# Issuing each product over a whole PSUM bank of 512 columns as two halves of 256 columns

## The chip, the cores and the metric

The kernel runs on one core of a Trainium2 chip. The metric is the device time of one execution in microseconds (us). The time before is the median of three runs: 1025.2 us (1024.93 to 1025.28).

## The reference

A gated scan over 6080 tokens of 256 features is followed by two feed-forward layers of 2048 hidden features, one with a leaky ReLU, one with an ELU. Everything is float32.

```python
sig = 1.0 / (1.0 + np.exp(-f_logit))
f = lower_bound + (1.0 - lower_bound) * sig
h = f[:, t] * h + (1.0 - f[:, t]) * x[:, t]     # for every t; y[:, t] = h
...
h = y @ w_in1;  g = np.maximum(0.01 * h, h);                                y = g @ w_out1
h = y @ w_in2;  g = np.where(h > 0.0, h, np.exp(np.minimum(h, 0.0)) - 1.0); out = g @ w_out2
```

## The kernel before

The tokens are worked in 12 chunks (`sizes`): eleven of 512 and, as the fifth, one of 448. Features lie on the partitions, tokens along the columns. A float32 operand is held as two parts in the type float32r, a high part (a rounded copy, made on ScalarE) and a low part (what the copy lost, made on VectorE). A product of two such operands takes three matmuls into the same place in PSUM: high by high, high by low, low by high. `mm3` (lines 572 to 577) issues these three; lines 575, 576 and 577 of the profile are they, for nearly every product of the kernel. The stationary operand of each matmul is a piece of 128 columns of a `w` tile, and each matmul loads it anew (PEld in the profile, LDWEIGHTS). The moving operand is an `act` tile (the input of a layer) or a `gate` tile (the activation's output).

`group(i)` (line 586) handles one entry of `stream`: a layer, a chunk and a quarter of the hidden features, that is two pairs of blocks of hidden features. It has two kinds of products.

- Products inward (`act` tiles). For most chunks `product` forms them by Strassen's scheme with seven products of half the size: the chunk's tokens are split in two halves, so that each matmul has 256 columns (224 in the chunk of 448). Each product is two calls of `mm3`, six matmuls, in one PSUM bank. The first two chunks of layer 1 are computed without the scheme (`plain`), with matmuls over 512 columns, because the combinations of the weights are not there yet.
- Products outward (`gate` tiles). `run` calls `mm3` for the two output blocks (`k`), each over the whole chunk: six matmuls of 512 columns (448 in the one chunk), into two banks. In the last chunk of layer 2 (`swapped`) the output is formed with the roles changed, the gate tile stationary and the weights moving, by lines 734 to 736, 256 columns each.

PSUM has eight banks, six `bank` tiles and two `seed` tiles; each holds 512 float32 columns. ScalarE and VectorE take the products out, apply the activation, and split the result into the high and low part of a gate tile (lines 704 and 707). At the start, VectorE, ScalarE and GpSimd also prepare the weights: they decode them from the words as loaded (lines 346 to 359) and split them (lines 371 and 373); line 463 and line 465 split the input of a plain chunk. While the first chunks run, the weights of layer 1 and the combinations of them are made in this way.

The order of the work on every engine is set by `Plan.emit`, a list scheduler that runs while the kernel is built. Each operation has a cost in microseconds, a due time and the operations that it waits for; the scheduler simulates the engines and issues, for each, the operation that can start and is due first. The costs of matmuls come from one function, which `cost_in` and `cost_out` use for the due times too:

```python
def mm(n):
    return n * 0.000451 + 0.0025
```

With it 256 columns cost 0.1180 us and 512 columns 0.2334 us.

Of the kernel before, what the change touches and what calls it, by code (L numbers as in the profile page):

```python
# [106 lines left out]
def kernel(  # L107
# [21 lines left out]
    nc = tc.nc  # L129
# [10 lines left out]
    CH = 512  # L140
# [29 lines left out]
    HC = CH // 2  # L170
# [24 lines left out]
        return 0.09 + n / 1200.0  # L195

    def mm(n):
        return n * 0.000451 + 0.0025

    DMA, LATE, FAR, SGN = 0.475, 2.3, 4.5, 0.8  # L200

# [25 lines left out]
    def cost_in(n):  # L227
        return 42 * mm(n // 2)

    def cost_out(n):  # L230
        return 24 * mm(n)
# [340 lines left out]
    def mm3(ps, wop, a, start, stop):  # L572


        nc.tensor.matmul(ps, wop[0], a[0], start=start, stop=False, skip_group_check=True)  # L575
        nc.tensor.matmul(ps, wop[0], a[1], start=False, stop=False, skip_group_check=True)  # L576
        nc.tensor.matmul(ps, wop[1], a[0], start=False, stop=stop, skip_group_check=True)  # L577

    y_in = {}
    prods = []  # L580
# [3 lines left out]
    def group(i):  # L584
# [24 lines left out]
        def product(bank, s, t, start, stop, after, **k):  # L609
            def run():  # L610
                for j, p in enumerate(pairs):
                    mm3(ps(bank)[:, j * h : (j + 1) * h], wop(p, s), src["op"](t), start and j == 0, stop)

            o = pe(6 * mm(h), due_in[i] + count[0] * step, run, after + src["done"][t] + wi + prods[-1:], **k)
            count[0] += 1
            prods.append(o)
            return o
# [8 lines left out]
        def plain():  # L626

            blocks = [(r, j) for r in (1, 0) for j in (0, 1)]
            todo = [(r, j, k) for r, j in blocks for k in range(KD)]
            if i < 2:  # L630
                todo.sort(key=lambda t: (t[2], t[1]) if i == 0 else t[2])
            for z, (r, j, k) in enumerate(todo):
                name = f"{r}{j}"

                def run(r=r, j=j, k=k, name=name):
                    s = {(1, 0): A11, (1, 1): A12, (0, 0): A21, (0, 1): A22}[r, k]
                    mm3(b[name][2][:, :n], wop(pairs[j], s), src["row"](k), k == 0, k == KD - 1)

                prods.append(pe(3 * mm(n), due_in[i] + z * step * 7 / 8, run,
                                wplain[pairs[j]] + src["rows"][k] + prods[-1:],  # L640
                                take=[(b, name, "seed" if j else "bank")] if k == 0 else [],
                                give=[(src, "p", "act")] if q == NQ - 1 and z == len(todo) - 1 else []))
                if k == KD - 1:
                    g = "hO" if r else "hE"
                    made.setdefault(r, []).append(act(s1(n), None, lambda j=j, name=name, g=g: nc.scalar.activation(
                        out=b[g][2][:, j * n : (j + 1) * n], in_=b[name][2][:, :n], func=AF.Prelu, alpha=0.01),
                        [prods[-1]], take=[(b, g, "h")] if j == 0 else [], give=[(b, name, "seed" if j else "bank")]))
# [69 lines left out]
        for z, (name, r, j) in enumerate(order):  # L717
            due = due_in[i] + 7 * step * (1.75 + z / 4)
            begin, end = q == 0 and z == 0, q == NQ - 1 and z == 3
            give = [(b, name, "gate")] if j == 1 else []  # L720

            def run(name=name, r=r, j=j, begin=begin, end=end):
                hi, lo = (gate(name, s)[:, j * n : (j + 1) * n] for s in (0, 1))
                wh, wl = wout(pairs[j], r)
                if not swapped:
                    for k in range(KD):
                        cols = slice(k * P, (k + 1) * P)
                        mm3(yb[k][2][:, :n], (wh[:, cols], wl[:, cols]), (hi, lo), begin, end)
                    return

                for t in range(n // P):
                    dst = yb[t // 2][2][:, t % 2 * D : (t % 2 + 1) * D]
                    ah, al = (s[:, t * P : (t + 1) * P] for s in (hi, lo))
                    nc.tensor.matmul(dst, ah, wh, start=begin and t % 2 == 0, stop=False, skip_group_check=True)  # L734
                    nc.tensor.matmul(dst, ah, wl, start=False, stop=False, skip_group_check=True)  # L735
                    nc.tensor.matmul(dst, al, wh, start=False, stop=end, skip_group_check=True)  # L736

            prev = pe(6 * mm(n), due, run, [gates[name], prev] + wo + outs[-1:],
                      take=[(yb, k, "bank") for k in range(KD)] if begin else [], give=give)
            outs.append(prev)  # L740
# [55 lines left out]
    for sd in seeds:  # L796
        for z in range(CH // P):
            nc.tensor.matmul(sd[:, z * P : (z + 1) * P], ident, ident, start=z == 0, stop=z == CH // P - 1,
                             skip_group_check=True)
# [67 lines left out]
```

## Time and profile before

| | |
|---|---|
| median of three runs | 1025.2 us |
| the profiled execution | 1024.31 us |
| its span, first to last instruction | 1022.5 us |
| mean granted TensorE clock | 0.996 |
| matmuls, and as many weight loads | 6336 |
| memory traffic | 47 MB read, 24 MB written, 69 GB/s over the span |

The profiled execution is 0.9 us shorter than the median; 1.8 us of it lie outside the span. PE is the matmul side of TensorE, PEld its weight loads, DVE is VectorE, ACT ScalarE, POOL GpSimd. A matmul's duration in the trace runs from its first read to a modelled end and overlaps the next matmuls, so the busy share of PE only tells that it had something in flight.

### The profile page before, as it was taken

Reading aid. Unit: us, or ns where it says so; the run is one execution under the profiler, and the core shown is the slowest. Engines: PE = TensorE matmul, PEld = TensorE weight load, DVE = VectorE, ACT = ScalarE, POOL = GpSimd, SP = SyncE. Lnnn points to the kernel's source line nnn. Section 1 sums busy time; section 2 is a strip of 40 time slices with the busy share of each in tenths; the row PEclk is TensorE's granted clock in tenths of the full one; section 3 lists DMA queues with packets and bytes.
Section 4 is the critical chain, followed back from the end, with each engine's and each line's share of the span. In section 5 each row is a group of like instructions: output and inputs, shape, how many; then the busy total and the mean of one; then the engine's idle time right before and its main releaser. Section 6 shows DMA issues by size and latency. Waiting matters only on the chain.

```text
span 1022.5 us, 15868 instructions
## 1 busy us (share of the span) xinstructions
PE 1009.5 (99%) x6336; PEld 901.7 (88%) x6336; DVE 758.5 (74%) x1061; ACT 714.9 (70%) x1038; POOL 36.6 (4%) x38
## 2 busy tenths in 40 slices
PE   7999999999999999999999999999999999999998
PEld 5777889999888888888898888889989888888997
DVE  7899867768779688474377776877777768787765
ACT  6776767777778677666577676766776767676664
POOL 2132000000000000000000000000000000000000
PEclk8999999999999999999999999999999999999999
DMA  6532333445264443211760201102102021021010
GB/s 185 134 104 62 76 90 93 129 98 140 59 150 104 124 93 103 40 50 40 281 214 2 42 1 39 42 1 43 27 14 42 1 42 42 2 42 16 7 21 21
DMA packets 155290, 71.99 MB, mean 70 GB/s; under 512 B 132176, under 2 KB 145488, under 8 KB 155216
## 3 DMA queue, kind: packets, MB, share of 16 engines
q1 hardware_dynamic: 155216, 70.98, 26.7%
q8 instruction: 49, 0.80, 0.3%
q14 instruction: 25, 0.20, 0.1%
HBM read 46.97 MB, written 23.99 MB: 69 GB/s over the span
## 4 chain that ended last, share of the span: by engine, by line
PE 89%; DVE 5%; ACT 2%; issue 2%; DMA 1%; SPq 1%; POOL 1%; DVEq 0%; ACTq 0%
PE bank L575 27%; PE bank L576 27%; PE bank L577 27%; PE seed L577 2%; PE seed L576 2%; PE seed L575 2%; DVE ws L359 1%; DVE ws L355 1%; ACT gate L704 1%; POOL ws L349 1%; DVE gate L707 1%; PE bank L736 1%; PE bank L734 0%; PE bank L735 0%; DVE w L373 0%
## 5 line engine op out<-in xcount | busy, mean ns | idle before, releaser
L575 PE MATMUL bank<-act,w 128*128 128x256 f32 (+2 forms) x1088 | 306.6, 282 | 0.4 <-ACT act L463 0.2
L576 PE MATMUL bank<-act,w 128*128 128x256 f32 (+2 forms) x1088 | 304.6, 280 | 1.3 <-DVE act L465 1.3
L577 PE MATMUL bank<-act,w 128*128 128x256 f32 (+2 forms) x1088 | 304.4, 280 | 0.0
L576 PE MATMUL bank<-gate,w 128*128 128x512 f32 (+1 forms) x736 | 289.1, 393 | 0.0
L577 PE MATMUL bank<-gate,w 128*128 128x512 f32 (+1 forms) x736 | 288.9, 393 | 0.0
L575 PE MATMUL bank<-gate,w 128*128 128x512 f32 (+1 forms) x736 | 287.9, 391 | 0.0
L623 DVE TENSOR_TENSOR h<-bank,sn 128x512 f32<-128x512 f32 (+1 forms) x176 | 120.3, 684 | 186.5 <-ACT sn L620 101.1
L576 PEld LDWEIGHTS bank<-act,w 128*128 128x128 f32 x1088 | 204.8, 188 | 18.5 <-DVE act L465 2.3
L575 PEld LDWEIGHTS bank<-act,w 128*128 128x128 f32 x1088 | 204.9, 188 | 17.6 <-ACT sn L620 1.1
L577 PEld LDWEIGHTS bank<-act,w 128*128 128x128 f32 x1088 | 204.7, 188 | 1.8 <-DVE w L373 0.5
L620 ACT COPY sn<-bank 128x512 f32<-128x512 f32 (+1 forms) x176 | 102.4, 582 | 105.0 <-PE bank L577 104.3
L577 PEld LDWEIGHTS bank<-gate,w 128*128 128x128 f32 x736 | 138.3, 188 | 29.7
L575 PEld LDWEIGHTS bank<-gate,w 128*128 128x128 f32 x736 | 138.4, 188 | 17.7
L576 PEld LDWEIGHTS bank<-gate,w 128*128 128x128 f32 x736 | 138.4, 188 | 16.0
L707 DVE TENSOR_TENSOR gate<-h,gate 128x1024 fp32r<-128x1024 f32 (+1 forms) x96 | 117.3, 1222 | 33.6 <-ACT gate L704 33.2
L707 DVE TENSOR_TENSOR gate<-ws,gate 128x1024 fp32r<-128x1024 f32 (+1 forms) x96 | 113.2, 1210 | 10.2 <-ACT gate L704 10.2
L704 ACT CAST gate<-h 128x1024 fp32r<-128x1024 f32 (+1 forms) x96 | 99.9, 1040 | 3.7 <-PE bank L577 1.9
L704 ACT CAST gate<-ws 128x1024 fp32r<-128x1024 f32 (+1 forms) x96 | 96.2, 1038 | 4.1 <-DVE ws L685 2.8
L679 ACT ACTIVATE ws<-bank 128x512 f32<-128x512 f32 (+1 forms) x48 | 28.5, 594 | 70.9 <-PE bank L577 70.9
L575 PE MATMUL seed<-act,w 128*128 128x256 f32 (+2 forms) x208 | 61.5, 296 | 0.8 <-ACT w L371 0.5
L577 PE MATMUL seed<-act,w 128*128 128x256 f32 (+2 forms) x208 | 61.4, 295 | 0.6 <-DVE w L373 0.4
L692 ACT ACTIVATE ws<-ws 128x1024 f32<-128x1024 f32 (+1 forms) x48 | 50.5, 1052 | 15.9 <-DVE ws L689 15.8
(72 smaller groups left out, 1159.9 us busy)
## 6 DMA issues: line engine op xcount, KB each, us to landing
ws<-in_moe_w_in_dram SPq DMA_DIRECT2D x32, 255.6 KB, 3.7
ws<-in_moe_w_out_dram SPq DMA_DIRECT2D x32, 255.6 KB, 3.5
w2d<-gate SPq DMA_DIRECT2D x8, 896.0 KB, 4.3
w<-w2d SPq DMA_DIRECT2D x8, 896.0 KB, 6.0
y1d<-t SPq DMA_DIRECT2D x22, 256.0 KB, 2.2
bt<-y1d SPq DMA_DIRECT2D x22, 256.0 KB, 2.9
out_dram<-t SPq DMA_DIRECT2D x80, 64.0 KB, 2.0
raw<-in_f_logit_dram SPq DMA_DIRECT2D x72, 64.0 KB, 3.1
```

Source lines behind the costliest of these rows:

```text
L349: sg = pool(SGN, None, lambda: nc.gpsimd.tensor_scalar(out=fr(), in0=top().bitcast(I8), scalar1=2.0, scalar2=-2.0, op0=ALU.min, op1=ALU.ma ...
L355: fm = dve(v1(n), None, lambda: nc.vector.scalar_tensor_tensor(out=fr().bitcast(I32), in0=mant(), scalar=5, in1=fr().bitcast(I32), op0=ALU ...
L359: mu = dve(v1(n), None, lambda: nc.vector.tensor_tensor(out=val()[:, :n], in0=fr(), in1=sc(), op=ALU.mult,), [fm, ex])
L575: nc.tensor.matmul(ps, wop[0], a[0], start=start, stop=False, skip_group_check=True)
L576: nc.tensor.matmul(ps, wop[0], a[1], start=False, stop=False, skip_group_check=True)
L577: nc.tensor.matmul(ps, wop[1], a[0], start=False, stop=stop, skip_group_check=True)
L620: return act(s1(2 * h), None, lambda: nc.scalar.copy(out=ps(name), in_=ps("X")), after, take=[(b, name, "sn")])
L623: return dve(v1(2 * h), None, lambda: nc.vector.tensor_tensor(out=half(name, s), in0=two(ps(bank)), in1=two(ps(sn)), op=ALU.add), after, **k)
L679: a, o = (act(s1(2 * h), None, lambda s=s, name=name: nc.scalar.activation(out=half("eO", s), in_=two(ps(name)), func=AF.Relu, scale=-1.0) ...
L692: e = act(s1(2 * n), None, lambda: nc.scalar.activation(out=whole("eE"), in_=whole("eE"), func=AF.Exp, scale=-1.0), [e])
L704: hi = act(s1(2 * n), None, lambda name=name, g=g: nc.scalar.copy(out=gate(name, 0), in_=whole(g)), done + highs[-1:], take=[(b, name, "ga ...
L707: gates[name] = dve(v1(2 * n), None, lambda name=name, g=g: nc.vector.tensor_tensor(out=gate(name, 1), in0=whole(g), in1=gate(name, 0).bit ...
```

## The change

`mm3` looks at the number of columns. Below 512 it issues its three matmuls as before. At 512 it issues the three for the columns 0 to 255 and then the three for the columns 256 to 511, into the same bank. Only the very first matmul of a bank carries the start mark. Each matmul loads its stationary operand itself, so the weight loads double with the matmuls. The cost function gets two new values, 0.1136 us for 256 columns and 0.2272 us for 512; other sizes keep theirs (448 columns 0.2045 us, 224 columns 0.1035 us).

```diff
--- before.py
+++ after.py
@@ -195,7 +195,7 @@
         return 0.09 + n / 1200.0
 
     def mm(n):
-        return n * 0.000451 + 0.0025
+        return (n * 0.000451 + 0.0025 if n < CH else 0.2272) if n != HC else 0.1136
 
     DMA, LATE, FAR, SGN = 0.475, 2.3, 4.5, 0.8
 
@@ -572,9 +572,12 @@
     def mm3(ps, wop, a, start, stop):
 
 
-        nc.tensor.matmul(ps, wop[0], a[0], start=start, stop=False, skip_group_check=True)
-        nc.tensor.matmul(ps, wop[0], a[1], start=False, stop=False, skip_group_check=True)
-        nc.tensor.matmul(ps, wop[1], a[0], start=False, stop=stop, skip_group_check=True)
+        n = ps.shape[-1]
+        parts = [slice(0, n)] if n < CH else [slice(0, HC), slice(HC, CH)]
+        for z, s in enumerate(parts):
+            nc.tensor.matmul(ps[:, s], wop[0], a[0][:, s], start=start and z == 0, stop=False, skip_group_check=True)
+            nc.tensor.matmul(ps[:, s], wop[0], a[1][:, s], start=False, stop=False, skip_group_check=True)
+            nc.tensor.matmul(ps[:, s], wop[1], a[0][:, s], start=False, stop=stop, skip_group_check=True)
 
     y_in = {}
     prods = []
```

The lines behind `mm3` move by three: 575 to 577 become 578 to 580, 704 and 707 become 707 and 710, 734 to 736 become 737 to 739. The program issues 8508 rows of work on TensorE instead of 6300. Since the scheduler works with other costs, the orders of the engines change too.

TensorE in layer 2, an output product of one quarter, before (`bank` tiles are PSUM banks, `gate` the moving operand, `w` the stationary one):

```order
L575 MATMUL bank_103<-gate_111,w_69 128x512
L576 MATMUL bank_103<-gate_111,w_69 128x512
L577 MATMUL bank_103<-gate_111,w_69 128x512
L575 MATMUL bank_104<-gate_111,w_69 128x512
L576 MATMUL bank_104<-gate_111,w_69 128x512
L577 MATMUL bank_104<-gate_111,w_69 128x512
```

and an output product of the same weights now, up to the first matmul of its second bank:

```order
L578 MATMUL bank_100<-gate_111,w_69 128x256
L579 MATMUL bank_100<-gate_111,w_69 128x256
L580 MATMUL bank_100<-gate_111,w_69 128x256
L578 MATMUL bank_100<-gate_111,w_69 128x256
L579 MATMUL bank_100<-gate_111,w_69 128x256
L580 MATMUL bank_100<-gate_111,w_69 128x256
L578 MATMUL bank_101<-gate_111,w_69 128x256
```

What were three matmuls into one bank are six of half the length, three for each half of the bank.

TensorE at the start of layer 1, in the second chunk (`act_107` is its input, `gate_109` the first gate tile of the first chunk), before:

```order
L575 MATMUL seed_99<-act_107,w_64 128x512
L576 MATMUL seed_99<-act_107,w_64 128x512
L577 MATMUL seed_99<-act_107,w_64 128x512
L575 MATMUL bank_105<-gate_109,w_63 128x512
L576 MATMUL bank_105<-gate_109,w_63 128x512
```

These three are the last plain matmuls of the second chunk's first quarter, and the first output product stood behind them. Now:

```order
L578 MATMUL bank_101<-gate_109,w_63 128x256
L579 MATMUL bank_101<-gate_109,w_63 128x256
L580 MATMUL bank_101<-gate_109,w_63 128x256
L578 MATMUL bank_104<-act_107,w_63 128x256
L579 MATMUL bank_104<-act_107,w_63 128x256
L580 MATMUL bank_104<-act_107,w_63 128x256
```

The first output product (its last rows are shown) stands ahead of the plain products that use the second half of the chunk's features.

VectorE at the same place (`act1` is the second chunk's input, `gate0` the first gate tile, `w1` a weight tile, `ws` scratch of the weights' preparation, `bt` and `t` tiles of the scan), before:

```order
L546 SCALAR_TENSOR_TENSOR bt0_108<-t2_129,last_h_94,t0_127 128x512
L359 TENSOR_TENSOR ws0_117<-ws0_117 128x512
L346 TENSOR_SCALAR up0_130<-ws1_118 128x512
L465 TENSOR_TENSOR act1_107<-bt0_108,act1_107 128x512
L355 SCALAR_TENSOR_TENSOR ws2_119<-ws1_118,ws2_119 128x512
L373 TENSOR_TENSOR w1_64<-ws0_117,w1_64 128x512
L707 TENSOR_TENSOR gate0_109<-h0_113,gate0_109 128x1024
```

and now:

```order
L546 SCALAR_TENSOR_TENSOR bt0_108<-t2_129,last_h_94,t0_127 128x512
L346 TENSOR_SCALAR up0_130<-ws1_118 128x512
L373 TENSOR_TENSOR w1_64<-ws0_117,w1_64 128x512
L710 TENSOR_TENSOR gate0_109<-h0_113,gate0_109 128x1024
L355 SCALAR_TENSOR_TENSOR ws0_117<-ws1_118,ws0_117 128x512
L465 TENSOR_TENSOR act1_107<-bt0_108,act1_107 128x512
```

The split of the second chunk's input (line 465) stood ahead of the split of the first gate tile and now stands behind it.

## Rows read from the trace of the kernel before

**Rows 1.** The page's head: span, then busy time of each engine and instructions.
```profile
span 1022.5 us, 15868 instructions
...
PE 1009.5 (99%) x6336; PEld 901.7 (88%) x6336; DVE 758.5 (74%) x1061; ACT 714.9 (70%) x1038; POOL 36.6 (4%) x38
```

**Rows 2.** Table of stretches, the first 100 us; columns as its first line says.
```profile
core 0: us, PE busy (x) PEld busy (x) DVE busy (x) ACT busy (x) POOL busy (x), PEclk, DMA share, GB/s
0.00:25.00 25.00, 19.00 (x81) 14.14 (x81) 17.54 (x28) 15.66 (x28) 5.16 (x11) 0.86 0.64 189
25.00:50.00 25.00, 24.11 (x102) 19.20 (x103) 21.52 (x30) 19.37 (x32) 4.09 (x5) 1.00 0.55 124
50.00:75.00 25.00, 24.85 (x107) 19.70 (x107) 24.44 (x46) 17.64 (x30) 8.42 (x4) 1.00 0.37 107
75.00:100.00 25.00, 24.09 (x103) 18.76 (x102) 24.43 (x50) 17.37 (x31) 6.72 (x3) 1.00 0.34 76
```

**Rows 3.** Table of stretches, TensorE alone: length, busy (count), clock, DMA, GB/s.
```profile
85.30:1011.50 926.20, 926.04 (x5964) 1.00 0.25 64
```

**Rows 4.** The chain that ended last, in order of time: start, length, engine and line.
```profile
84.51 0.61 DVE w L373
85.17 0.50 PE seed L577
```

**Rows 5.** Groups of matmuls by shape, whole span: count | busy us, mean ns | idle before.
```profile
L575 PE MATMUL bank<-act,w 128*128 128x256 f32 x960 | 267.3, 278 | 0.2
...
L575 PE MATMUL bank<-gate,w 128*128 128x512 f32 x672 | 264.4, 393 | 0.0
L575 PE MATMUL seed<-act,w 128*128 128x256 f32 x160 | 44.2, 276 | 0.0
...
L734 PE MATMUL bank<-w,gate 128*128 128x256 f32 x64 | 17.8, 278 | 0.0
...
L575 PE MATMUL bank<-act,w 128*128 128x512 f32 x32 | 13.2, 414 | 0.2 <-ACT act L463 0.2
...
L575 PE MATMUL seed<-act,w 128*128 128x512 f32 x32 | 12.9, 404 | 0.8 <-ACT w L371 0.5 <-ACT h L645 0.3
```

**Rows 6.** The same groups in the first 85.4 us.
```profile
L575 PE MATMUL bank<-gate,w 128*128 128x512 f32 x42 | 16.6, 396 | 0.0
...
L575 PE MATMUL bank<-act,w 128*128 128x512 f32 x26 | 10.9, 418 | 0.2 <-ACT act L463 0.2
...
L575 PE MATMUL seed<-act,w 128*128 128x512 f32 x25 | 10.2, 407 | 0.8 <-ACT w L371 0.5 <-ACT h L645 0.3
```

**Rows 7.** Timeline of TensorE in layer 2: start us, duration us, instruction.
```profile
799.76 0.39 PE L575 MATMUL bank<-gate,w 128*128 128x512 f32 x1
...
801.15 0.28 PE L575 MATMUL bank<-act,w 128*128 128x256 f32 x1
...
802.52 0.39 PE L575 MATMUL bank<-gate,w 128*128 128x512 f32 x1
```

**Rows 8.** The same view, where every matmul has 512 columns, to the first of 256.
```profile
86.21 0.39 PE L575 MATMUL bank<-act,w 128*128 128x512 f32 x1
...
101.61 0.28 PE L575 MATMUL bank<-act,w 128*128 128x256 f32 x1
```

**Rows 9.** The same view, in the chunk of 448 tokens.
```profile
700.30 0.27 PE L575 MATMUL bank<-act,w 128*128 128x224 f32 x1
...
701.63 0.37 PE L575 MATMUL bank<-gate,w 128*128 128x448 f32 x1
...
702.85 0.27 PE L575 MATMUL bank<-act,w 128*128 128x224 f32 x1
```

**Rows 10.** The same view, in the last chunk of layer 2.
```profile
984.84 0.28 PE L575 MATMUL bank<-act,w 128*128 128x256 f32 x1
...
987.67 0.28 PE L575 MATMUL bank<-act,w 128*128 128x256 f32 x1
...
990.40 0.28 PE L575 MATMUL bank<-act,w 128*128 128x256 f32 x1
```

## The prediction

> **What bounds the kernel now.** I read the page's head first: TensorE is busy 99% of a span of 1022.5 us, no other engine above 88%, and that one is its own weight load [rows 1]. Then the table of stretches: in the first 100 us TensorE lacks about 8 us and VectorE is busy for 24.4 of 25 us from 50 us on [rows 2]. From 85.3 to 1011.5 us TensorE misses only 0.2 us, with a granted clock of 1.00, the 2.4 GHz level [rows 3]. The chain of waits agrees: VectorE's split of a weight ends it at 85.17 us, and the chain's next step is a matmul [rows 4]. So up to 85 us the time is set by VectorE's preparation, and from there to the end by the distance from one matmul's start to the next. A matmul's own duration in the trace is no measure of that, since matmuls overlap: 0.39 us is printed for one, while six start within 1.39 us [rows 7]. I therefore use starts only.
>
> **The price of one matmul.** In the steady state six matmuls over 512 columns run from 799.76 to 801.15 us and the twelve of 256 columns behind them to 802.52 us [rows 7]: 1.39 / 6 = 231.7 ns and 1.37 / 12 = 114.2 ns. The borders blur this a little: the first of each kind is early or late by some nanoseconds. A stretch with 512 columns alone is cleaner: 66 matmuls from 86.21 to 101.61 us are 15.40 / 66 = 233.3 ns each [rows 8], whether they read an act tile or a gate tile. So the higher price belongs to the length, not to the operand. For the pair of kinds, the whole period of six and twelve is 2.76 us; six at 233.3 are 1.40 us, which leaves 1.36 / 12 = 113.3 ns for 256 columns. Two of those are 226.7 ns, 6.7 ns less than one of 512. Why the longer one costs more per column no row tells.
>
> **The change, part by part.**
>
> *More matmuls.* Per line there are 672 matmuls of 512 columns out of the gate tiles and 32 + 32 out of act tiles [rows 5]; over three lines 2208. Each becomes two, with a weight load of its own each. 42 + 26 + 25 = 93 per line, 279 in all, start before 85.4 us [rows 6], where TensorE waits for VectorE; their 279 x 6.7 ns = 1.9 us I count as nothing, since VectorE's busy stretch covers it, and if that cover were gone they would be a further gain. The other 1929 lie on the path: 1929 x 6.67 ns = **12.9 us less**. The 3360 matmuls that have 256 columns already (960 + 160 per line) keep their price, and so do those of 448 and 224, which the new code leaves whole, and the last chunk's 192 (64 per line, written apart).
>
> *Their weights.* 2208 more weight loads run beside matmuls. The nearest row that shows a limit is the chunk of 448 tokens: twelve matmuls of 224 columns take from 700.30 to 701.63 us, 110.8 ns each, and six of 448 from there to 702.85, 203.3 ns each [rows 9]. Half of 203.3 would be 101.7, so at 224 columns something that doesn't shrink with the columns, most likely the load that each carries, sets about 111 ns. 113.3 is 2.5 ns above it. In the nearest row, the runs of twelve [rows 7], that suffices, and I take the extra loads at nothing. The bound on the other side is a slip of the pace to 117.9 ns, which the last chunk shows (the first rival).
>
> *Other order, up to 85 us.* The planner's cost falls from 0.1180 to 0.1136 us for 256 columns and from 0.2334 to 0.2272 for 512, so it sets other orders. At the start two things move: the first output product stands ahead of half of the second chunk's first-layer products on TensorE, and on VectorE the split of that chunk's second operand (line 465) goes behind the first gate's (line 707). TensorE there waits for whichever is late; nothing in the trace shows the new wait. From below: nothing, or a gain, as the other product fills time in which TensorE waited. From above: the moved product's own length, 1.4 us, twice over. The next thing that is late is VectorE's chain to 85.17 us, which has the same work in it. I take zero and keep 3 us to either side.
>
> *Other order, behind 85 us.* The alternation of six and twelve stays. VectorE and ScalarE get 1.3% less time for the same work, with 74% and 70% busy [rows 1]; nothing. If a wait does come back, it is for a gate split or for a PSUM copy; I leave 2 us for it in the range.
>
> The sum: 1024.31 us for the profiled execution, less 12.9, is 1011.4. The median of the runs is 1025.2, 0.9 above that execution, so the forecast is **1012.3 us**. Its own range is 1007 (with the 1.9 us of the start and 3 of order) to 1017.
>
> *A rule that speaks against it.* By rows, two halves save 6.7 ns [rows 7, 8]. The Trainium skill, page "TensorE: Matmul & The Clock Gate", section "Back-to-back issue gap", gives a warm gap of N / 2.4 + 2.5 ns, a fixed part in each matmul, so that cutting one in two adds 2.5 ns; by it the sum would be 1025.2 + 1929 x 2.5 ns = 1030.0 us, an estimate. The trace doesn't agree for either length: 233.3 where the page has 215.8, 113.3 where it has 109.2, and the whole costs more than its halves.
>
> **The rivals.**
>
> *The pace slips (slower).* The last chunk is the one place with 256 columns and nothing else, output products among the others, and it runs at two paces: 24 matmuls from 984.84 to 987.67 us, 117.9 ns each, then 24 to 990.40 us, 113.8 ns [rows 10]. The slow pace begins and ends where a first-layer-type product follows an output product, and holds through both kinds. In the steady state a run of 512s stands between such places, and the products behind it are fast; the change takes the 512s away. Place: every stretch behind 85 us. Price: 2 x 1929 + 3360 = 7218 matmuls at 4.6 ns if all are slow, 33 us; half of them, as in the last chunk, 17, so 1012.3 + 17 = **1029 us**; all of them 1045. It decides from 12.9 / 33 = 39% slow matmuls on. Against it: in the last chunk the roles are swapped (the gate tile is the stationary side), which the changed loop doesn't do, and in the runs of twelve products no border between two products brings the slow pace.
>
> *A fixed price in each half (slower).* If the new halves run at 117.9 ns and the old products stay at 113.3, a pair costs 235.8, 2.5 ns more than the whole: 1929 x 2.5 ns = 4.8, **1030 us**. For it: halving 448 does cost here, 2 x 110.8 - 203.3 = 18 ns [rows 9]. Against it: 256 columns are measured, not 224. The page's rule above gives the same time by another road.
>
> *It saves nothing (same).* The price goes by columns whoever reads them, and the halves of a gate tile take 116.7 ns each: **1025 us**. Against it: at 512 columns act and gate cost the same [rows 8], so at 256 they should too.
>
> **How the numbers follow.** Forecast 0.60; the slip 0.26 (0.05 of it with all slow); the fixed price 0.07; nothing saved 0.07. About 0.2% (2 us) is what a measurement can tell from no change. Faster: the forecast and those slips that stay below a third, 0.64. Within: nothing saved and slips near 39%, 0.09. Slower: 0.27. The range runs from 1007 to 1031 and leaves out slips above one half and a start worse than allowed, some 2 in 10.
>
> **What would show it.** Right: with 8544 matmuls on TensorE, twelve halves of an output product take 1.36 us in the steady state (1.39 before), the period of six and twelve becomes 2.72 us, and TensorE has no gaps behind some 85 us. The slip: stretches of 12 or 24 at 118 ns, beginning behind an output product. The fixed price: only the halves at 118. Nothing saved: halves at 117, products at 113. A wrong step of order: the first unbroken stretch of TensorE begins well after 85 us, or waits for VectorE stand behind it.

## The result

The changed kernel takes 1014.7 us in the median of four executions (1010.36 to 1017.36), the kernel before 1025.24 (1024.93 to 1026.21). The ratio is 0.9891, 95% interval 0.9856 to 0.9927: 1.1% faster, at 2.4 us above the forecast and inside its range. The kernel before stayed within 1.3 us; this one spreads over 7 us, and most of what follows is about that. The profiled execution is the shortest of the four, 1010.36 us.

The page's head of the changed kernel, to be read against [rows 1]:

```profile
span 1008.4 us, 20290 instructions
...
PE 993.6 (99%) x8544; PEld 987.8 (98%) x8544; DVE 759.2 (75%) x1061; ACT 713.5 (71%) x1038; POOL 35.2 (3%) x38
```

The span is 14.1 us shorter, with 2208 more matmuls. TensorE's timeline in the steady state, at the first matmul of two output and two inward products (each row shown is the first of its twelve):

```profile
400.53 0.28 PE L578 MATMUL bank<-gate,w 128*128 128x256 f32 x1
...
401.89 0.28 PE L578 MATMUL bank<-act,w 128*128 128x256 f32 x1
...
403.25 0.28 PE L578 MATMUL bank<-gate,w 128*128 128x256 f32 x1
...
404.61 0.28 PE L578 MATMUL bank<-act,w 128*128 128x256 f32 x1
```

Twelve take 1.36 us, of either kind, 113.3 ns each, and a period of 24 is 2.72 us, where [rows 7] had 2.76. To see where the 14.1 us come from, take two marks that both timelines have: the first matmul of the chunk of 448 in layer 1, and the first of the swapped output in the last chunk. Before:

```profile
184.77 0.26 PE L575 MATMUL bank<-act,w 128*128 128x224 f32 x1
...
983.48 0.28 PE L734 MATMUL bank<-w,gate 128*128 128x256 f32 x1
```

After:

```profile
182.60 0.27 PE L578 MATMUL bank<-act,w 128*128 128x224 f32 x1
...
969.34 0.28 PE L737 MATMUL bank<-w,gate 128*128 128x256 f32 x1
```

2.2 us are won by the first mark and 12.0 between the two. In the kernel before, 1668 matmuls of 512 columns lie between the marks (from the groups by shape of that stretch); at the forecast's 6.67 ns they are 11.1 us, and the period above confirms that price (2.76 - 2.72 us over six of them). The other 0.9 us are starts that come late in the kernel before, nine of them between 241 and 357 us with 1.0 us in all. Here two follow each other, 0.36 and 0.22 us behind the start ahead of them instead of 0.11:

```profile
356.40 0.28 PE L577 MATMUL bank<-act,w 128*128 128x256 f32 x1
356.76 0.38 PE L575 MATMUL bank<-act,w 128*128 128x256 f32 x1
356.98 0.28 PE L576 MATMUL bank<-act,w 128*128 128x256 f32 x1
```

The profile of the changed kernel has no such start in that stretch. Behind the second mark nothing is won (39.1 us in both).

The start did change its shape. TensorE's list of waits:

```profile
PE bank L579 <- DVE gate L710: 2.4, 1, 2.4
...
PE bank L578 <- ACT sn L623: 0.9, 1, 0.9
```

The first is the moved output product at 25.8 us, which waits for the low part of its gate tile. The second is late: from 61 us on the chain of waits runs mostly over VectorE, with steps of ScalarE, SyncE's queue and one DMA, until here,

```profile
107.73 0.48 ACT sn L623
108.25 0.38 PE bank L578
```

that is until 108 us, not 85 [rows 4]. That VectorE's preparation reaches further because TensorE is quicker is likely, but was not tried by itself. Behind it TensorE has no wait until the last chunk.

### The profile page after: what moved, and what is told of

It reads as the page before. It is cut to its first block, busy times and chain, and to the rows that moved or that the text cites. A ratio compares the mean times of both kernels' runs of the same rounds, so it can differ in the third digit from the quotient of the medians.

```text
span 1008.4 us, 20290 instructions
## 1 busy us (share of the span) xinstructions
PE 993.6 (99%) x8544; PEld 987.8 (98%) x8544; DVE 759.2 (75%) x1061; ACT 713.5 (71%) x1038; POOL 35.2 (3%) x38
## 4 chain that ended last, share of the span: by engine, by line
PE 91%; DVE 5%; ACT 1%; issue 1%; DMA 1%; SPq 1%; DVEq 0%
PE bank L580 28%; PE bank L578 28%; PE bank L579 28%; PE seed L580 2%; PE seed L579 2%; PE seed L578 2%; DVE gate L710 1%; PE bank L739 1%; PE bank L737 0%; PE bank L738 0%; DMA ws<-in_moe_w_in_dram 0%; DVE bt L546 0%; DVE w L373 0%; DVE h L253 0%; SPq L521 0%
## 5 line engine op out<-in xcount | busy, mean ns | idle before, releaser
L579 PE MATMUL bank<-gate,w 128*128 128x256 f32 (+1 forms) x1408 | 394.6, 280 | 2.4 <-DVE gate L710 2.4
L578 PE MATMUL bank<-gate,w 128*128 128x256 f32 (+1 forms) x1408 | 394.7, 280 | 0.0
L580 PE MATMUL bank<-gate,w 128*128 128x256 f32 (+1 forms) x1408 | 394.3, 280 | 0.0
L578 PE MATMUL bank<-act,w 128*128 128x256 f32 (+1 forms) x1120 | 309.6, 276 | 1.7 <-ACT sn L623 0.9
L579 PE MATMUL bank<-act,w 128*128 128x256 f32 (+1 forms) x1120 | 309.4, 276 | 0.7 <-DVE act L465 0.7
L580 PE MATMUL bank<-act,w 128*128 128x256 f32 (+1 forms) x1120 | 309.3, 276 | 0.7 <-DVE w L373 0.7
L579 PEld LDWEIGHTS bank<-gate,w 128*128 128x128 f32 x1408 | 264.5, 188 | 3.0 <-DVE gate L710 2.6
L580 PEld LDWEIGHTS bank<-gate,w 128*128 128x128 f32 x1408 | 264.4, 188 | 0.9
L578 PEld LDWEIGHTS bank<-gate,w 128*128 128x128 f32 x1408 | 264.4, 188 | 0.5
L578 PEld LDWEIGHTS bank<-act,w 128*128 128x128 f32 x1120 | 210.7, 188 | 2.8 <-ACT act L463 1.3
L579 PEld LDWEIGHTS bank<-act,w 128*128 128x128 f32 x1120 | 210.6, 188 | 1.5 <-DVE act L465 1.1
L580 PEld LDWEIGHTS bank<-act,w 128*128 128x128 f32 x1120 | 210.6, 188 | 1.0 <-DVE w L373 1.0
L710 DVE TENSOR_TENSOR gate<-ws,gate 128x1024 fp32r<-128x1024 f32 (+1 forms) x96 | 113.3, 1211 | 9.8 <-ACT gate L707 9.8
L578 PE MATMUL seed<-act,w 128*128 128x256 f32 (+1 forms) x240 | 66.3, 276 | 0.0
L579 PE MATMUL seed<-act,w 128*128 128x256 f32 (+1 forms) x240 | 66.2, 276 | 0.0
L580 PE MATMUL seed<-act,w 128*128 128x256 f32 (+1 forms) x240 | 66.2, 276 | 0.0
```

Of the source, the lines that this page charges most:

```text
L578: nc.tensor.matmul(ps[:, s], wop[0], a[0][:, s], start=start and z == 0, stop=False, skip_group_check=True)
L579: nc.tensor.matmul(ps[:, s], wop[0], a[1][:, s], start=False, stop=False, skip_group_check=True)
L580: nc.tensor.matmul(ps[:, s], wop[1], a[0][:, s], start=False, stop=stop, skip_group_check=True)
L710: gates[name] = dve(v1(2 * n), None, lambda name=name, g=g: nc.vector.tensor_tensor(out=gate(name, 1), in0=whole(g), in1=gate(name, 0).bit ...
```

## The experiments

**The same kernel again.** No edit.

> The changed kernel once more, to see where its spread of 7 us between executions comes from (1010.4 to 1017.4 us, where the kernel before stayed within 1.3 us). Theory: the steady state is the same in all executions (113.33 ns per matmul of 256 columns), and an execution that takes 1014 to 1017 us loses the 4 to 7 us in the first 110 us, where TensorE waits for gates and weights. Rival: the slow pace of some 118 ns takes hold of stretches behind 110 us in some executions; 5 us would be some 1100 matmuls at 4.6 ns more. If the profiled execution is a long one, its timeline decides; if it is again about 1010 us, only the spread is confirmed.

Four executions, 1013.47 to 1016.57 us, median 1014.5; the profiled one took 1014.06. The table of stretches, first of the execution of 1010.36 us, then of this one. Its columns are the stretch, its length, busy time with the number of matmuls, the clock, and DMA; the number includes two or three that were in flight as the stretch began.

```profile
30.00:70.00 40.00, 40.00 (x356) 1.00 0.49 132
120.00:170.00 50.00, 50.00 (x443) 1.00 0.45 112
250.00:300.00 50.00, 50.00 (x443) 1.00 0.45 126
400.00:500.00 100.00, 100.00 (x885) 1.00 0.33 103
```

```profile
30.00:70.00 40.00, 40.00 (x342) 1.00 0.50 132
120.00:170.00 50.00, 50.00 (x426) 1.00 0.44 113
250.00:300.00 50.00, 50.00 (x444) 1.00 0.43 116
400.00:500.00 100.00, 100.00 (x885) 1.00 0.29 88
```

Same program, same order, no gap in either, granted clock 1.00 in both: yet 443 matmuls in 50 us in one execution and 426 in the other (113.4 and 117.9 ns, taking two off each count), with the DMA as busy in one as in the other, and from the chunk of 448 on both are alike. The theory (a loss at the start by waits) falls; the rival (the slow pace holds) stands, but from 28 to 187 us, where it was looked for behind 110. Less the waits that this execution doesn't have, it costs 3.9 us of span, by which that chunk begins later here. The pace is there right behind the 2.4 us wait: from 28.4 us on the starts are 113 ns apart in the one execution and 118 ns in the other, and stay so.

The spread has a second part, which other profiles show. Ten profiles have the wait for the first gate, with 2.3 to 2.8 us from the start ahead of it to the start behind it. In four of them (the costs alone, six in each quarter, six a chunk and the short chunk early, all below) the granted clock fell to 0.50, the 1.2 GHz level, behind that wait. The same stretch of the run with the short chunk early, then of the changed kernel:

```profile
28.60:32.00 3.40, 3.32 (x15) 0.50 0.47 144
```

```profile
28.60:32.00 3.40, 3.40 (x31) 1.00 0.47 163
```

Sixteen matmuls fewer, at 113 ns, are 1.8 us. The four profiles of the old order (the kernel before and three of the split alone) have no distance of starts above 1.3 us behind 25 us, and no such fall. Of the changed kernel's eight executions, three have a mean clock of 0.997 or 0.998 and take 1010.36 to 1014.06 us; the five with 0.994 or 0.995 take 1014.45 to 1017.36. None of the five was profiled: that this fall is in them is likely and not shown.

**The split alone, old costs.**

```diff
-        return (n * 0.000451 + 0.0025 if n < CH else 0.2272) if n != HC else 0.1136
+        return n * 0.000451 + 0.0025
```

> The split alone: halves of 256 columns, but the planner's costs as before (0.1180 and 0.2334 us), so the old order. Theory (the saving is 6.67 ns in each split matmul, and the new order is worth nothing): 1012 us, with TensorE paced at 113.33 ns in the steady state. Rival (the new order has a part in the gain): 1016 us or more. For the spread: if the new order at the start makes it, this kernel stays within 1.5 us as the kernel before did.

Twelve executions from 1014.86 to 1031.65 us, median 1025.51, in the median no better than the kernel before; without the three longest the ratio is 0.9959 (0.9929 to 0.9988). The profiled one was the shortest. Two more executions were profiled:

> The split with the planner's old costs, whose twelve executions lay between 1014.9 and 1031.7 us; one more look to catch a long one in a profile. Theory: a long execution has the slow pace, 117.8 ns, over one of the three stretches between the chunks of 448 and the ends: from the start to 185 us (some 4 us), from 222 to 674 us (some 17 us) or from 712 to 974 us (some 10 us); so about 1015, 1025 or 1031 us. Rival: waits behind VectorE or ScalarE, with gaps on TensorE and the pace at 113.3.

> As the look before it: the same kernel again. A long execution shows by the theory whole stretches of 117.8 ns, by the rival gaps.

They took 1019.21 and 1031.13 us. The last in the table of stretches:

```profile
250.00:300.00 50.00, 50.00 (x434) 1.00 0.44 115
350.00:400.00 50.00, 49.94 (x424) 1.00 0.42 106
400.00:500.00 100.00, 100.00 (x852) 1.00 0.20 58
800.00:900.00 100.00, 100.00 (x885) 1.00 0.11 22
```

852 matmuls in 100 us against 885, at full occupation: 117.7 ns each. Its timeline shows where this slow pace begins:

```profile
327.25 0.28 PE L580 MATMUL bank<-act,w 128*128 128x256 f32 x1
327.61 0.39 PE L578 MATMUL bank<-act,w 128*128 128x256 f32 x1
327.83 0.28 PE L579 MATMUL bank<-act,w 128*128 128x256 f32 x1
327.94 0.28 PE L580 MATMUL bank<-act,w 128*128 128x256 f32 x1
```

One start comes 0.36 us behind the one before it, and the next again 0.22, instead of 0.11 to 0.12. In that execution late starts stand at 253, 284 to 285, 327 and 359 to 360 us. Behind 285 the pace is slow, from 317 quick again without a late start, and from 328 slow until the next chunk of 448 at 691 us. The late starts at 359 and 360 us changed nothing: the pace was slow ahead of them,

```profile
328.50:358.50 30.00, 30.00 (x257) 1.00 0.39 99
```

and in the execution of 1014.86 us the quick pace came through late starts at 282, 313, 324 and 355 us. So the new costs do have a part in the gain, and the time of the late starts themselves, 1 us in the kernel before, is the small part of it: with the old ones such starts stay behind the first chunk of 448, and each may, but need not, set off hundreds of microseconds at the slow pace.

**The new costs alone.**

```diff
-        return n * 0.000451 + 0.0025
+        return (n * 0.000451 + 0.0025 if n < CH else 0.2272) if n != HC else 0.1136
```

(to the kernel before)

> The planner's new costs alone, matmuls of 512 columns whole as before. Theory: 1025 us within 2, since TensorE is bound by the distance of its matmuls and that is 233.3 ns as before; the start may be some us better or worse. Rival (the order makes the gain): 1018 us or less.

1024.58 us, eleven executions from 1022.46 to 1025.32; ratio 0.9988 (0.9979 to 0.9997). That is within the theory's band: the order alone is worth some 1 us, which is what the late starts of the kernel before come to (this profile has 0.2 us of them, at 243 us). Without the split the executions stay within 3 us.

**Halves of 224 as well.**

```diff
-        parts = [slice(0, n)] if n < CH else [slice(0, HC), slice(HC, CH)]
+        parts = [slice(0, n)] if n < 448 else [slice(0, n // 2), slice(n // 2, n)]
```

> Split the 192 matmuls of 448 columns as well, in halves of 224. Theory (a floor of some 111 ns under each matmul with its own weight load): a pair costs 222 ns where the whole costs 203.3, so 192 x 18.4 ns = 3.5 us more than the changed kernel run beside it. Rival (halves always save 6.7 ns): 1.3 us less. In the chunk of 448 the halves should stand 111 ns apart, by the rival 98.

1017.95 us (1017.25 to 1019.41), 3.45 above the 1014.5 of the changed kernel, which spreads over 3 us itself: near the theory's 3.5, and the timeline is the better witness. In that chunk:

```profile
204.96 0.28 PE L578 MATMUL bank<-gate,w 128*128 128x224 f32 x1
...
206.30 0.27 PE L578 MATMUL bank<-act,w 128*128 128x224 f32 x1
```

Twelve halves take 1.34 us, 111.7 ns each, where six of 448 took 1.22 [rows 9]. So there is a floor, and 256 columns clear it by 2 ns. The Trainium skill, page "TensorE: Matmul & The Clock Gate", section "LDWEIGHTS (loading the stationary operand)", gives a load as its columns / 1.2 ns, 106.7 for 128, an estimate that lies 5 ns under this floor; the trace prints 188 ns for one load, but the loads overlap. That the load is what sets the floor was not tried by itself.

**No changed roles in the last chunk.**

```diff
-        swapped = l == 2 and c == NC - 1
+        swapped = False
```

> The changed kernel with the last chunk of layer 2 written out as the other chunks (weights stationary, gate tile moving, transposed on VectorE) instead of with the roles changed. Theory: the slow pace in the last chunk comes from the changed roles; without them that chunk runs at 113.3 ns throughout, some 0.6 us faster in its matmuls, and the end gets longer by the transposed writing. Rival (any border between output products and products can bring it): the last chunk still has stretches of 118 ns.

1015.43 us (1013.28 to 1017.47), no gain. But in the stretch from 968 to 990 us, in the last chunk, it has 197 matmuls and the changed kernel, in the second row, 192:

```profile
968.00:990.00 22.00, 22.00 (x197) 1.00 0.17 26
```

```profile
968.00:990.00 22.00, 22.00 (x192) 1.00 0.17 26
```

Without the changed roles the quick pace holds there, so what [rows 10] shows at the borders of products belongs to those roles. The rival that I had built on these rows was right about the two paces; in the main part hundreds of such borders pass without a change of pace.

**Three whole matmuls in each quarter.** The thought was to have a longer matmul bring the quick pace back, as 512 columns seemed to do in the kernel before.

```diff
-        parts = [slice(0, n)] if n < CH else [slice(0, HC), slice(HC, CH)]
+        parts = [slice(0, n)] if n < CH or whole else [slice(0, HC), slice(HC, CH)]
...
-                        mm3(yb[k][2][:, :n], (wh[:, cols], wl[:, cols]), (hi, lo), begin, end)
+                        mm3(yb[k][2][:, :n], (wh[:, cols], wl[:, cols]), (hi, lo), begin, end, whole=z == 3 and k == KD - 1)
```

> The changed kernel, but in each quarter the last three of the output product's matmuls stay whole (512 columns): 84 quarters x 3 = 252 matmuls. Theory: the stream of 256-column matmuls has two paces that hold themselves, 113.33 and 117.8 ns, and takes the fast one behind longer matmuls, as it did behind 448 columns in the last profile and behind 512 columns all over the kernel before. Then no slow stretch is longer than one quarter (some 10 us), the 252 cost 252 x 6.67 ns = 1.7 us against an all-fast execution of 1010.4, so 1012 to 1013 us, with a spread of at most 1.5 us. Rival (a wait at the start chooses the pace and longer matmuls don't set it back): 1016 us with the spread of 3 to 7 us that the changed kernel has.

1027.35 us (1026.09 to 1028.10), ratio 1.0020 (1.0012 to 1.0029): the theory missed by 15 us. The whole ones stand at 394.43 and 405.01 us. The stretches of halves behind the one group and behind the next:

```profile
395.20:404.30 9.10, 9.10 (x79) 1.00 0.01 2
405.80:415.20 9.40, 9.40 (x85) 1.00 0.79 189
```

118 ns, then 113, and so on through the kernel: a group of three exchanges the paces. About half of the matmuls are then slow. The spread left is 2 us, and it goes with the mean clock: five executions at 0.997 or 0.998 take 1026.09 to 1027.02 us, six at 0.995 1027.35 to 1028.10.

**Six whole matmuls, in each quarter or once a chunk.**

```diff
-mm3(yb[k][2][:, :n], (wh[:, cols], wl[:, cols]), (hi, lo), begin, end, whole=z == 3 and k == KD - 1)
+mm3(yb[k][2][:, :n], (wh[:, cols], wl[:, cols]), (hi, lo), begin, end, whole=z == 3)
```

(to the kernel of the run before, in each quarter; once a chunk with `z == 3 and q == NQ - 1`)

> As the run with three whole matmuls a quarter, but six: both output blocks of a quarter's last output product stay whole, 84 x 6 = 504 matmuls of 512 columns, 504 x 6.7 ns = 3.4 us more than all halves at the fast pace. Three a quarter exchanged the two paces from quarter to quarter. Theory A (behind six, as all over the kernel before, the fast pace comes whatever stood ahead): no slow stretch outlasts a quarter, 1014 us within 1, with a spread of at most 1.5 us. Theory B (an even number leaves the pace that was there, and only a wait or the chunk of 448 sets it anew): 1014 to 1020 us, spread over 3 to 7 us like the changed kernel's, and the profile shows a slow stretch that goes on behind a group of six.

> Six whole matmuls only in the last quarter of each chunk: 21 x 6 = 126 matmuls, 0.8 us more than all halves at the fast pace. By theory A of the run beside it slow stretches end with their chunk: 1011 to 1013 us, spread of 2 us or less, below the changed kernel's median of 1014.5. By theory B nothing but 0.8 us more than the changed kernel: 1015 us, spread as there.

In each quarter: 1015.12 us (1014.19 to 1015.36). The spread is A's; the time lies 0.1 us above A's band and inside B's. Its profile has one slow stretch, behind a wait at 110 us, and it ends at the next six (the stretches ahead of them and behind them):

```profile
111.64:117.29 5.65, 5.65 (x51) 1.00 0.12 19
118.69:127.50 8.81, 8.81 (x79) 1.00 0.43 103
```

Once a chunk: 1011.32, 1011.36, 1012.05, 1013.01 and 1017.94 us, ratio 0.9874 (0.9857 to 0.9890), the lowest median of all. But the profiled execution was the one of 1017.94:

```profile
50.00:100.00 50.00, 50.00 (x427) 1.00 0.33 85
120.00:170.00 50.00, 50.00 (x420) 1.00 0.41 107
250.00:300.00 50.00, 50.00 (x437) 1.00 0.45 112
```

Its slow pace goes on behind the six at 108 us (and at 119 and 161) until the chunk of 448, which A excludes. So neither holds: one group of six ended a slow stretch, three others left it. The lower median may be chance at the start of five executions. The one of 1017.94 also has the fall of the clock at 29 us.

**Other lengths.**

```diff
-        parts = [slice(0, n)] if n < CH else [slice(0, HC), slice(HC, CH)]
+        cut = (320, 384)[next(turn) % 2]
+        parts = [slice(0, n)] if n < CH else [slice(0, cut), slice(cut, CH)]
```

> The cut of each whole-bank product put elsewhere, by turns behind column 320 and behind column 384, so that the trace shows starts for 320, 192, 384 and 128 columns. Theory (a start-to-start distance of 0.469 ns per column less 6.7 ns, through 113.3 ns at 256 columns and 233.3 at 512, with a floor of 111 ns from the weight load): 143 ns behind 320 columns, 173 behind 384, 111 behind 192 and behind 128. Pairs of 254 and 284 ns against 233.3, so 2208 pairs with 27 to 58 ns more each less what the start hides: 1100 to 1125 us. Rival (0.4557 ns per column at any length and a floor of 107): 146 and 175 ns.

1111.3 us, one execution. The timeline:

```profile
465.96 0.34 PE L582 MATMUL bank<-gate,w 128*128 128x384 f32 x1
...
466.31 0.22 PE L581 MATMUL bank<-gate,w 128*128 128x128 f32 x1
...
468.16 0.31 PE L582 MATMUL bank<-gate,w 128*128 128x320 f32 x1
...
468.45 0.25 PE L581 MATMUL bank<-gate,w 128*128 128x192 f32 x1
```

The first pair of rows are two matmuls of 384 columns, 175 ns each, the second two of 320, 145 ns; over all of them behind 120 us the second and third of a triple take 147 and 176 to 177 ns. That is the rival's 146 and 175, not 143 and 173: about 0.46 ns per column, as at 512 (0.456) and as 256 columns have at the slow pace (117.8 / 256 = 0.460). The quick pace, 0.443, is what stands out. Matmuls of 192 and 128 columns follow each other after 106 to 113 ns, but for the first of a triple.

**The short chunk earlier.**

```diff
-        sizes.insert(4, rest)
+        sizes.insert(2, rest)
```

> The changed kernel with its chunk of 448 tokens as the third instead of the fifth. In every profile of a split kernel so far the fast pace stands behind that chunk. Theory (a wait of TensorE draws one of two paces, which then holds; the chunk of 448 ends it): the stretch that can be slow ends near 140 us instead of 222 us, in both layers, which leaves some 80 us x 4% x one half = 1.5 us less in the median than the changed kernel's 1014.5, so 1013 us, spread of 4 us or less, as long as no new wait follows behind the chunk. Rival (the pace behind the chunk is chance, too): median and spread as the changed kernel's, with slow stretches behind 140 us in the profile.

Seven executions: four from 1009.97 to 1013.62, three from 1022.20 to 1025.24; median 1013.62, and without the longest a ratio of 0.9900 (0.9867 to 0.9933). With two such groups, a median near the theory's 1013 us says little. The profiled one is of the second group. Its timeline and table of stretches:

```profile
326.97 0.28 PE L580 MATMUL bank<-gate,w 128*128 128x256 f32 x1
327.18 0.38 PE L578 MATMUL bank<-act,w 128*128 128x256 f32 x1
327.40 0.28 PE L579 MATMUL bank<-act,w 128*128 128x256 f32 x1
```

```profile
250.00:300.00 50.00, 50.00 (x444) 1.00 0.46 125
350.00:400.00 50.00, 50.00 (x427) 1.00 0.40 105
400.00:500.00 100.00, 100.00 (x851) 1.00 0.25 77
700.00:800.00 100.00, 100.00 (x885) 1.00 0.13 28
```

Ahead of 327 us the pace is quick. Two starts come 0.1 us late each, and from there to the chunk of 448 at 601 us it is slow: 0.2 us of delay, and 274 us at 4% more, 10 us. The condition in the expectation, no new wait behind the chunk, was not met, and by that estimate its price is most of the 12 us between the two groups of executions; the other two of the longer group were not profiled. Behind the chunk of 448 the pace is quick again, as in every profile of a split kernel here.

## Why the prediction was right, and where not

*The price of a half* was right. 113.3 ns holds through all-256 stretches of hundreds of microseconds, on gate and act tiles alike. Of the 14.1 us of the profiled execution 12.9 are the forecast's halves, 1929 at 6.67 ns. With it the rule of a fixed part in each matmul falls for these matmuls, which carry a load each, as do the rivals of a fixed price and of nothing saved.

*The weights' loads* were right to be costed at nothing at 256 columns while the quick pace holds, and the bound from the rows of 224 was confirmed by the run that halves 448.

*The start* was taken at zero with 3 us to either side. In its place the wait for the first gate cost 2.4 us, and VectorE's chain lasted to 108 us instead of 85; the sum at 183 us is still 2.2 us to the good, of which 261 halves are 1.7. The start itself is thus near the zero that was taken for it, in this execution; where the clock falls behind the wait, it is 1.8 us worse.

*The order behind 85 us* was taken at nothing, on the ground that VectorE and ScalarE have time to spare. It is worth 0.9 us: the late starts between 241 and 357 us, small as they are in the rows of the kernel before, had been overlooked, and the new order is without them.

*"If a wait does come back", 2 us in the range*, is the step that was mis-sized. The waits are as small as thought. What I didn't see is that a wait can decide the pace of all that follows up to the next chunk of 448. In its two profiles the changed kernel has them ahead of that chunk, and then in the last chunk only; the one at the slow pace lost 3.9 us. With 1.8 us for the fall of the clock that is 5.7 us, an estimate that covers most of the spread of 7 us and the 2.4 us from 1012.3 to 1014.7; the longest execution has no profile. With the old costs or the short chunk moved, late starts stand behind that chunk, and 10 to 17 us go. So it is luck, as far as the forecast goes, that the new costs left none there: by the same reasoning the split with the old costs would have been put at 1012 us, and its median was 1025.5.

*The slip* had the right price (117.8 ns against 117.9 taken) and the right form, whole stretches at 118. Its trigger was wrong: most changes of pace stand not at any border of an output product but at a late start, or at a group of three longer matmuls. A few stand at neither: at 39 us in the execution of 1014.86 us a single distance of 123 ns leads from the quick pace to the slow one. In the kernel before, a slow matmul stood in the steady state nearly always directly behind the groups of 512, so its rows had no long stretch to show it, but for the last chunk.

## What to carry to other kernels

Price a matmul by the distance between starts in a dense stretch, at each length that the kernel has, and not by its printed duration or by columns alone: here 256 columns cost less than half of 512, and 224 (111 ns) nearly as much as 256. A bound engine with two stable paces makes a kernel's time depend on its few small waits, so read counts per stretch in several executions before you believe a median. Take a scheduler's costs from the measured pace: here a plan that was 4% off (0.1180 us for 0.1133) left late starts that the right costs did not leave.

## What the runs showed of the hardware

A dense stream of float32r matmuls over 256 columns, each with its own weight load, ran at 113.3 or at 117.8 ns with the granted clock at 1.00 in both. Most changes from one to the other stood at starts that came late by 0.1 to 2.7 us, though many such starts changed nothing and several changes stood at a distance of 120 to 184 ns only; the slow pace stayed for up to 363 us. Three matmuls of 512 columns exchanged the two, and the chunk with 224 and 448 columns left the quick one behind in every profile of a kernel split at 256. In four of ten profiles a wait of some 2.5 us on TensorE was followed by matmuls at the 1.2 GHz level, 213 ns apart for 256 columns. What in the chip holds the pace, and why six of 512 end it once and not another time, stays open. Why 0.46 ns per column is paid at 320 to 512 columns and 0.443 in the quick stream was not found either.
